# A one-core decode step (cached attention beside a gated MLP): z in 8 products per chunk, four wo chunks into the first accumulator, w_out dealt anew

## The chip, the cores and the metric

The kernel runs on 1 core of one Trainium2 chip. The metric is device time in microseconds (us) of one execution. Before the change it is 662.26 us (median of 3 runs, 662.09 to 662.38).

## The reference

For 4 batch rows of width 640, x is layer-normed to xn, and the result is x + attention(xn) + mixer(xn).

```python
q = (xn @ wq)                       # 640 -> 32 heads x 128, one query per row
p = softmax(q . k_cache / sqrt(128))  # k_cache: 4 x 32 x 4096 x 128, bf16
o = p . v_cache                     # v_cache: the same shape
A = o.reshape(4, 1, 4096) @ wo      # 4096 -> 640

z  = gelu_tanh(xn @ w_in)           # 640 -> 1728
z1, z2 = z[:, :864], layernorm(z[:, 864:])
B  = (z1 * (w_sp * z2 + b_sp)) @ w_out   # 864 -> 640; w_sp is 1 x 1, b_sp one number
out = x + A + B
```

The two caches are 134 MB each; wq, wo and the mixer's weights come to some 14 MB.

## The kernel before, in words

**Units.** The heads are taken in 4 groups of 8 (`NG`, `HG`), the batch rows one by one, so there are 16 units of K and 16 of V, 8.4 MB each: 128 partitions with 64 KB each. A tile `kv` of five slots of 32 KB per partition holds what is in flight; `place` (L159 to L166) says which two slots a unit takes. The sequence `seq` is K of units 0 to 3, then V and K in turn. `load_unit` (L179) issues a unit's load on SyncE's queue (SP), in one DMA or in the pieces of `cuts`. SP's queue is in order: a load waits for its slot to be free, and everything behind it waits too.

**K.** `emit_K` (L409) transposes an eighth of a unit on VectorE (L420, L429) into `kT_t`, a part of the tile `w_words`, and multiplies it on TensorE (L434) into the score tile S in PSUM. After the fourth K unit of a group, `softmax` makes p, and `z_fill` (L454) spreads it into `Zb`, also in `w_words`. `emit_V` (L497) multiplies V by it (L505).

**The prologue.** SP issues wq (slot 0 and 1) and w_in (slot 2), then pieces "a" and "b" of w_out (`load_piece`, L139), then K of unit 0. GpSimd's queue (POOL) issues a small load into the tile `walk` (L133) and the pieces "w", "s", "n", "m", "l" of w_out, each held behind the one before by `tc.issue_after`. w_out lies in `w_words` before K's transposes may write there: 95 partitions by `FC` = 26 columns of 640 numbers (a chunk of the contraction for each column). `PC` gives for each piece the partitions p0 to p1 with step st, the first chunk, the number of chunks n, and k and run, which say how the rows of w_out in DRAM are laid over partitions and chunks: `(r i c) n -> i r (c n)`, with i = k and c = run. Partitions that no piece covers stay zero from the memsets of L135 and L136.

**z.** For each of the 5 chunks of the contraction over 640, L343 multiplies xn by the columns of w_in in the order in which w_out's rows lie over partitions and chunks: 16 products per chunk (for pieces with `run == n`, one for each r), 80 in all, into two banks of PSUM (`zr_ps`), in six blocks of 32 partitions (`z_in`). The gelu (L351, ScalarE, 8 instructions) writes them into `z_f`, whose halves are z1 and z2. The layer norm's sums, the normalisation, the gate and the product run on VectorE and GpSimd (L363 to L381) over 32 * FC = 832 columns; L382 transposes the result in 32 x 32 blocks to `uT`. L395 multiplies it with w_out: 26 chunks by 2 halves of the output, 52 products into the accumulator `proj`, which already holds x (L288). K's first transpose may write `w_words` only after them.

**Slots.** w_in and z_f lie in slot 2. K of unit 2 goes to slots 2 and 3, so that its load waits for the product of L381 and for the transposes of K of unit 0 out of slot 3.

**The end.** Behind the last V, SP issues wo: groups 1, 2 whole and the last group (`NG - 1`) in pieces of chunks 0 to 4, 4 to 6, 6 to 7 and 7 to 8 (`load_wo`, L192). `emit_proj` (L551, its products at L548) adds groups 0 to 2 into `proj`, even chunks into rows 0 to 31 and odd ones into rows 32 to 63. The last accumulation into `proj` is that of group `NG - 2`, chunks 4 to 8. VectorE copies one half (`o_1`, L601) and adds the other (`o_q`, two instructions of L605). The last group's 8 chunks go by quarters of the output, 32 products, into an accumulator of their own, `last` (L608 to L613). L616 adds `last` and `o_q`, and two DMAs (L619) write the result.

**The walk.** Five loads of 4 bytes into `walk` (L569) stand on SP's queue between the loads of K of units 0 and 1, each waiting for an earlier DMA.

Of the kernel before, what the change touches and what calls it, by code (L numbers as in the profile page):

```python
# [8 lines left out]
ACT = mybir.ActivationFunctionType  # L9
# [3 lines left out]
BF16 = mybir.dt.bfloat16  # L13
# [3 lines left out]
def kernel(  # L17
# [19 lines left out]
    nc = tc.nc  # L37
# [5 lines left out]
    HG = 8  # L43
# [8 lines left out]
    NG = H // HG  # L52
# [1 line left out]
    G = HG * B  # L54
    F2 = B_w_in.shape[1]
    Fh = F2 // 2
    FC = 26

    PC = {"a": (32, 52, 2, 0, 18, 5, 18), "b": (0, 12, 1, 0, 14, 3, 14), "w": (16, 28, 2, 0, 19, 3, 19),
          "s": (60, 68, 1, 0, 23, 2, 23), "n": (68, 84, 2, 0, 17, 4, 17), "m": (84, 92, 2, 0, 1, 2, 1),
          "l": (92, 95, 1, 0, 26, 2, 13)}
    f_of, f_end = {}, 0
    for t, (p0, p1, st, _, n, _, _) in PC.items():
        f_of[t] = (f_end, f_end + len(range(p0, p1, st)) * n)
# [4 lines left out]
    NO2 = NOUT // NH  # L71
# [3 lines left out]
    const = ctx.enter_context(tc.tile_pool(name="const", bufs=1))  # L75
# [12 lines left out]
    def misc_ps(shape, dtype):  # L88
        misc_ctr[0] += 1
        return ps_m.tile(shape, dtype, tag="misc", name=f"misc{misc_ctr[0]}")  # L90
# [8 lines left out]
    n_w = (2 * NKT, (2 * TC + 1) * 16, NW * HG * 2, NW * HG * 2, NP // 2 + M)  # L99
    w_words = const.tile([P, max(sum(n_w), FC * NOUT // 2)], F32, name="w_words")  # L100
    w_part = [w_words[:, sum(n_w[:i]):sum(n_w[:i + 1])] for i in range(len(n_w))]
# [27 lines left out]
    w_in = at_slot(2, n_in).rearrange("p (c f) -> p c f", c=DC)  # L129
    nc.sync.dma_start(out=w_in, in_=B_w_in.rearrange("(p c) f -> p c f", c=DC))  # L130

    walk = const.tile([8, 138], BF16)
    sw = nc.gpsimd.dma_start(out=walk[:, 0:128], in_=B_w_out[0:8, 0:128].rearrange("(r i) n -> i r n", i=4))  # L133
    MS = 15 * NOUT // 2
    nc.vector.memset(w_words[:, 0:MS], 0.0)  # L135
    nc.gpsimd.memset(w_words[:, MS:FC * NOUT // 2], 0.0)  # L136
    w_out = w_words[:, 0:FC * NOUT // 2].bitcast(BF16).rearrange("p (c n) -> p c n", c=FC)

    def load_piece(eng, t):  # L139
        p0, p1, st, c0, n, k, run = PC[t]  # L140
        return eng.dma_start(out=w_out[p0:p1:st, c0:c0 + n].rearrange("p c n -> p (c n)"),
                             in_=B_w_out[f_of[t][0]:f_of[t][1], :].rearrange("(r i c) n -> i r (c n)", i=k, c=run))

    load_piece(nc.sync, "a")
    load_piece(nc.sync, "b")
    for t in ("w", "s", "n", "m", "l"):
        with tc.issue_after(sw.ins):
            sw = load_piece(nc.gpsimd, t)

    NB = 32 * FC  # L150
    z_at = n_in
# [117 lines left out]
    for q in range(4):  # L269
        nc.gpsimd.tensor_copy(out=SelE[32 * q:32 * q + 32, :, q % 2, :],  # L270
                              in_=b8[32 * q:32 * q + 32, 8:8 + HP, None].to_broadcast((32, HP, P // HG)))
# [10 lines left out]
                          in_=ident_f[:].rearrange("p (q x c) -> p q x c", q=2, c=C2))  # L282


    proj = ps_j.tile([64, 512], F32)
# [8 lines left out]
    for hf in range(2):  # L294
        for c in range(DC):
            for j in range(NG):
                n0 = j * HG * Dh + hf * 512
# [16 lines left out]
    w_z = w_in.rearrange("p c (a f) -> p c a f", a=2)  # L314
    zr_ps = [misc_ps([P, 2, 256], F32) for _ in range(2)]
# [2 lines left out]
    z_in = {(0, 0): ('b',), (0, 1): ('a',), (0, 2): ('n', 'm', 'l'), (1, 0): ('w',), (1, 1): ('s',), (1, 2): ('s',)}  # L318
    z_at_col, z_parts = {}, []
    for (bk, q), names in z_in.items():  # L320
        col, parts = 0, []
        for t in names:
            p0, p1, st, _, n, k, run = PC[t]
            x0, x1 = max(p0, 32 * q), min(p1, 32 * q + 32)
            m = len(range(x0, x1, st)) * n
            assert col + m <= 256
            src = w_z[:, :, :, f_of[t][0]:f_of[t][1]].rearrange("p d a (r i c) -> p d a r i c", i=k, c=run)
            dst = zr_ps[bk][32 * q:32 * q + 32, :, col:col + m]
            if x1 - x0 < p1 - p0:
                parts.append((dst, src[:, :, :, :, (x0 - p0) * k // (p1 - p0)]))  # L330
            elif run < n:
                d_i = dst.rearrange("p a (i f) -> p i a f", i=k)
                parts += [(d_i[:, i], src[:, :, :, :, i]) for i in range(k)]
            else:
                d_r = dst.rearrange("p a (i r c) -> p r a i c", i=k, c=n)
                parts += [(d_r[:, r], src[:, :, :, r]) for r in range(m // (k * n))]
            z_at_col[bk, q, t] = (col, m, n, PC[t][3], x0 - 32 * q, x1 - 32 * q, st)
            col += m
        z_parts.append(parts)
    for c in range(DC):  # L340
        for parts in z_parts:
# [4 lines left out]
    z_b = [ppool.tile([P, NB], BF16, tag="p", name=f"z_b{i}") for i in range(2)]  # L346
    zT = z_f[:, 0:2, :].rearrange("p a (i j) -> p a i j", j=32)
    nc.gpsimd.memset(z_f[:, 0:2, :], 0.0)
    for (bk, q, t), (col, m, n, c0, x0, x1, st) in z_at_col.items():
        rows = slice(32 * q, 32 * q + 32)  # L350
        nc.scalar.activation(out=zT[rows, :, c0:c0 + n, x0:x1:st],  # L351
                             in_=zr_ps[bk][rows, :, col:col + m].rearrange("p a (x c) -> p a c x", c=n),
                             func=ACT.Gelu_apprx_tanh)

    one_bf = const.tile([1, P], BF16)
    nc.vector.memset(one_bf[:], 1.0)
# [32 lines left out]

    for f0 in range(0, FC, 4):  # L390
        for hf in range(NH):
            for fc in range(f0, min(f0 + 4, FC)):
                nb = 32 if fc == 1 and hf == 0 else RW
# [139 lines left out]
    def emit_oT(g):  # L533
        om = state.pop(("om", g))
        oR = small.tile([P, B, HG], F32, tag="oR")
        nc.vector.tensor_reduce(out=oR[:], in_=om[:].rearrange("p b q c -> p b c q"), axis=AX.X, op=ALU.add)
        oT = small.tile([P, HG * RW + 2], BF16, tag="oT", bufs=3)
        nc.gpsimd.memset(oT[:], 0.0)  # L538
        nc.vector.tensor_tensor(out=oT[:, 1:1 + HG * RW].rearrange("p (c b h) -> p c b h", c=HG, h=NH)[:, :, :, 0],
                                in0=oR[:].rearrange("p b c -> p c b"),  # L540
                                in1=state.pop(("rinv", g))[:, None, :].to_broadcast((P, HG, B)), op=ALU.mult)
        state[("oT", g)] = oT

    def o_mul(dst, g, c, hf, n0, n1, start, stop):

        nb = 32 if start else RW
        c0 = RW * c + 1 - hf
        nc.tensor.matmul(dst[0:nb, 0:n1 - n0], lhsT=state[("oT", g)][:, c0:c0 + nb], rhs=wo_t[g][:, c, n0:n1],  # L548
                         start=start, stop=stop)

    def emit_proj(g, h2=range(2), stop=False):  # L551
        for h in h2:
            for hf in range(NH):
                for c in range(4 * h, 4 * h + 4):
                    o_mul(proj[32 * (c % 2):32 * (c % 2) + 32], g, c, hf, hf * NO2, (hf + 1) * NO2, False,
                          stop and hf == NH - 1 and c > HG - 3)
# [6 lines left out]
    for i, item in enumerate(seq):  # L563
# [13 lines left out]
        g, b = divmod(u, B)  # L577
# [17 lines left out]
    emit_sel(NG - 1)  # L595
    emit_proj(NG - 2, (0,))
    emit_oT(NG - 1)
    emit_proj(NG - 2, (1,), True)

    o_1 = ppool.tile([32, NO2], F32, tag="p", name="o_1")  # L600
    nc.vector.tensor_copy(out=o_1[:], in_=proj[0:32, 0:NO2])  # L601
    NQ = NO2 // 2
# [2 lines left out]
        nc.vector.tensor_tensor(out=o_q[32 * k:32 * k + 32, :], in0=proj[32:64, k * NQ:(k + 1) * NQ],  # L605
                                in1=o_1[:, k * NQ:(k + 1) * NQ], op=ALU.add)
    last = ps_l.tile([64, NQ], F32)
    for c in range(HG):  # L608
        for hf in range(NH):
            for k in range(2):  # L610
                n0 = hf * NO2 + k * NQ
                o_mul(last[32 * k:32 * k + 32], NG - 1, c, hf, n0, n0 + NQ, c == 0 and hf == 0,
                      c == HG - 1 and hf == NH - 1)  # L613

    o_bf = ppool.tile([64, NQ], BF16, tag="p", name="o_bf")
# [32 lines left out]
```

## Time and profile before

| | us |
|---|---|
| median of 3 runs (range) | 662.26 (662.09 to 662.38) |
| the profiled execution, its own time | 662.32 |
| its span, first to last instruction | 660.5 |
| TensorE / VectorE / ScalarE / GpSimd busy | 277.2 / 377.4 / 74.8 / 76.9 |
| bytes read from HBM | 282.25 MB, 427 GB/s over the span |
| granted TensorE clock, mean | 0.75 |

The profile shows one execution. Engines are PE (TensorE), PEld (its weight loads), DVE (VectorE), ACT (ScalarE), POOL (GpSimd) and SP (SyncE); a name with q is an engine's queue. The span is cut in 40 slices of 16.5 us; a digit of 9 is a busy share of 90% or more. The chain that ended last is followed back from the last instruction, each time to what released it. Times in the timeline are from the span's start; behind an instruction stands in brackets how long its engine was idle and what ended that. Beside the instructions the trace holds one record for each DMA packet (start, duration, bytes, queue) and one for each landing of a DMA on one of the 16 DMA engines; the numbers on single packets come from these.

### The profile page before, as it was taken

The page shows a single profiled execution, that of the slowest core. Times are in us where ns is not written, and L with a number is a line of the kernel's source. Part 1 is how long each engine was busy: PE and PEld are TensorE (multiplying, and loading weights), DVE is VectorE, ACT ScalarE, POOL GpSimd, SP SyncE. Part 2 cuts the span into 40 slices and gives each one's busy share as a digit, 9 for nine tenths or more (in the row PEclk, how much of TensorE's full clock was granted, in tenths as well). Part 3 has the DMA queues.
Part 4 walks back from the last instruction along what each step waited for, and adds up shares of the span by engine and source line. Part 5 has one row for each costly group of instructions (what it writes and reads, how often), then busy time and mean ns, then how long its engine had stood idle before and what let it go on. Part 6 is the DMA issues. An engine that isn't in the chain of part 4 may idle for free.

```text
span 660.5 us, 5606 instructions
## 1 busy us (share of the span) xinstructions
PE 277.2 (42%) x2329; PEld 106.6 (16%) x2329; DVE 377.4 (57%) x316; ACT 74.8 (11%) x144; POOL 76.9 (12%) x138
## 2 busy tenths in 40 slices
PE   0435566436052445334335062444507244244246
PEld 0222111112011121111112021111202112011012
DVE  4239999756191759718356192886619175485112
ACT  0310000431100000330200000033100000006200
POOL 7441000031100000130300000003110000003300
PEclk9759878668687697667859577776957779596769
DMA  9999999999999999999999999999999999999997
GB/s 369 444 446 442 407 430 439 441 438 437 426 425 442 429 420 443 438 426 437 434 429 441 442 417 434 433 433 438 438 429 433 418 437 442 433 442 433 400 433 309
DMA packets 6796, 282.60 MB, mean 428 GB/s; under 512 B 1080, under 2 KB 1344, under 8 KB 1602
## 3 DMA queue, kind: packets, MB, share of 16 engines
q1 hardware_dynamic: 6392, 281.58, 98.9%
q0 software_dynamic: 352, 0.66, 0.3%
q8 instruction: 18, 0.29, 0.2%
q14 instruction: 6, 0.05, 0.0%
q10 hardware_dynamic: 28, 0.01, 0.0%
HBM read 282.25 MB, written 0.01 MB: 427 GB/s over the span
## 4 chain that ended last, share of the span: by engine, by line
DMA 70%; DVE 12%; issue 12%; PE 3%; POOL 1%; ACT 1%; SPq 0%; DVEq 0%; POOLq 0%; ACTq 0%
DMA kv<-in_A_k_cache_dram 59%; DVE w_words L420 10%; DMA kv<-in_A_v_cache_dram 4%; DMA kv<-in_B_w_in_dram 4%; DMA kv<-in_A_wo_dram 4%; PE O L505 1%; PE proj L395 1%; DVE w_words L429 1%; POOL kv L379 0%; PE misc L343 0%; ACT kv L351 0%; DVE w_words L485 0%; POOL z_b L381 0%; SPq L194 0%; PE S L434 0%
## 5 line engine op out<-in xcount | busy, mean ns | idle before, releaser
L420 DVE STREAM_TRANSPOSE w_words<-kv 128x2048 f32<-128x2048 f32 x124 | 273.8, 2274 | 131.8 <-DMA kv<-in_A_k_cache_dram 128.7
L434 PE MATMUL S<-w_words,QZ 128*32 128x512 bf16 x1024 | 176.2, 473 | 269.0 <-DVE w_words L420 267.5
L434 PEld LDWEIGHTS <-QZ 128*32 128x32 bf16 x1024 | 57.3, 107 | 386.6 <-issue 324.5
L505 PE MATMUL O<-kv,w_words 128*32 128x512 bf16 x1024 | 72.0, 443 | 50.4 <-DMA kv<-in_A_v_cache_dram 40.6
L471 ACT ACTIVATE w_words<-w_words,MkE 32x128 bf16<-32x128 bf16 x120 | 60.9, 508 | 100.9 <-PE O L505 87.7
L514 DVE TENSOR_TENSOR om<-O,Mk 128x512 f32<-128x512 f32 x15 | 10.4, 692 | 83.8 <-PE O L505 83.8
L469 POOL TENSOR_SCALAR w_words<-w_words,MkE 32x128 bf16<-32x128 bf16 x60 | 43.1, 718 | 122.6 <-PE O L505 102.0
L479 ACT ACTIVATE w_words<-S,negmax 128x1024 bf16<-128x1024 f32 x4 | 4.5, 1114 | 413.1 <-DVE negmax L451 413.1
L505 PEld LDWEIGHTS <-w_words 128*32 128x32 bf16 x1024 | 32.8, 109 | 88.5 <-issue 59.0
L467 DVE TENSOR_SCALAR w_words<-w_words,MkE 32x128 bf16<-32x128 bf16 x76 | 24.9, 327 | 2.3
L403 POOL COPY QZ<-qT 32x32 bf16<-32x32 bf16 x16 | 5.0, 315 | 178.2 <-PE S L434 177.6
L515 DVE TENSOR_REDUCE R<-om 128x128 f32<-128x512 f32 x15 | 15.3, 1021 | 0.5
L490 POOL TENSOR_SCALAR rs<-MkB,rowsum 128x4 f32<-128x4 f32 x4 | 1.2, 296 | 120.8 <-ACT w_words L479 120.8
L485 DVE STREAM_TRANSPOSE w_words<-w_words 128x1024 bf16<-128x1024 bf16 (+1 forms) x8 | 9.6, 1240 | 5.6 <-ACT w_words L479 5.6
L538 POOL MEMSET oT<- 128x66 bf16 x4 | 0.5, 152 | 97.8 <-PE proj L548 97.8
L395 PE MATMUL proj<-w_words,z_b 128*8 128x320 bf16 (+1 forms) x52 | 6.5, 440 | 8.8 <-DVE z_b L382 8.8
L429 DVE STREAM_TRANSPOSE w_words<-kv 128x1024 f32<-128x1024 f32 x8 | 9.3, 1201 | 0.0
L517 DVE TENSOR_SCALAR R<-O,Mk 128x128 f32<-128x128 f32 x1 | 0.4, 351 | 12.7 <-PE O L505 12.7
L527 PE MATMUL misc<-R,SelX 128*128 128x512 f32 x8 | 4.5, 644 | 7.1 <-DVE R L515 5.5
L441 DVE TENSOR_REDUCE m<-S 128x1 f32<-128x1024 f32 x4 | 4.9, 1224 | 4.0 <-PE S L434 4.0
L298 PE MATMUL q<-kv,xnT 128*32 128x512 bf16 x40 | 4.5, 630 | 6.2 <-DMA walk<-in_B_w_out_dram 6.2
L492 PE MATMUL misc<-rs,SelE 128*128 128x4 f32 x8 | 2.3, 364 | 10.4 <-POOL rs L490 10.4
(102 smaller groups left out, 97.6 us busy)
## 6 DMA issues: line engine op xcount, KB each, us to landing
kv<-in_A_k_cache_dram SPq DMA_DIRECT2D x4, 4096.0 KB
kv<-in_A_v_cache_dram SPq DMA_DIRECT2D x1, 6144.0 KB
kv<-in_A_wq_dram SPq DMA_DIRECT2D x1, 5120.0 KB
kv<-in_A_wo_dram SPq DMA_DIRECT2D x3, 1280.0 KB
kv<-in_B_w_in_dram SPq DMA_DIRECT2D x1, 2160.0 KB
kv<-in_A_v_cache_dram SPq DMA_DIRECT2D x1, 2048.0 KB
kv<-in_A_wo_dram SPq DMA_DIRECT2D x1, 640.0 KB
kv<-in_A_wo_dram SPq DMA_DIRECT2D x1, 320.0 KB
```

The source lines that it names most:

```text
L395: nc.tensor.matmul(proj[r0:r0 + nb, 0:NO2], lhsT=uT[:, u0:u0 + nb], rhs=w_out[:, fc, hf * NO2:(hf + 1) * NO2], start=(fc == 1 and hf == 0) ...
L403: nc.gpsimd.tensor_copy(out=QZ[r0:r0 + 32, :, :, :, 8 + 8 * hp], in_=qT[32 * g:32 * g + 32, NE * hp:NE * hp + NE].rearrange("p e a b -> p ...
L420: nc.vector.transpose(kT.rearrange("p (t r) -> p t r", r=32), kw)
L429: nc.vector.transpose(kT_v[:, x], kw[:, TC * x:TC * x + TC])
L434: nc.tensor.matmul(S_ps[32 * q:32 * q + 32, i], lhsT=QZ[:, b, 2 * kh + w, e, w0:w0 + 32], rhs=kb[:, i, :, e, :, w], start=(b == 0 and k < ...
L467: nc.vector.tensor_scalar(out=dst, in0=src, scalar1=mk, scalar2=None, op0=ALU.mult)
L469: nc.gpsimd.tensor_scalar(out=dst, in0=src, scalar1=mk, scalar2=None, op0=ALU.mult)
L471: nc.scalar.activation(out=dst, in_=src, func=ACT.Copy, scale=mk)
L485: nc.vector.transpose(pT_t[:, j0:j1, :], blocks)
L505: nc.tensor.matmul(O_ps[32 * q:32 * q + 32, :, :], lhsT=Zb[b % 2][:, w].rearrange("p h c -> p (h c)"), rhs=vv[:, w * 4 * Dh:(w + 1) * 4 * ...
L514: nc.vector.tensor_tensor(out=om4[:], in0=O_ps[:], in1=Mk4[:, :, None].to_broadcast((P, 4, Dh)), op=ALU.mult)
L515: nc.vector.tensor_reduce(out=R, in_=om4[:].rearrange("p c d -> p d c"), axis=AX.X, op=ALU.add)
```

## The change

Three things, and what follows from them.

1. *w_out is dealt anew.* `FC` goes from 26 to 24. Piece b takes 13 chunks in place of 14, w 18 in place of 19, s 24 in place of 23, l 24 in place of 26; a and n stay. m was 4 partitions by 1 chunk (4 rows of w_out) and becomes 1 partition by 20 chunks (20 rows). Ahead of m a load of 256 bytes into `walk` is put on POOL's queue. All of the mixer's instructions over 32 * FC columns go from 832 to 768, and L395 from 52 to 48 products.
2. *z in 8 products per chunk.* For pieces with `run == n` the products no longer follow the order of the chunks; neighbouring pieces of one block are multiplied in one product, in the order of w_in's columns. The gelu reads the PSUM in permuted order; where the permutation has too many dimensions for one instruction it is two, one for each half of z: 12 gelus in place of 8 (b, a, n and w have two each).
3. *The end.* The chunks 0 to 4 of the last wo group go into `proj`, in 8 products of 320 columns; `o_1` and `o_q` follow behind these. `last` takes chunks 4 to 8, 16 products in place of 32.

```diff
--- before.py
+++ after.py
@@ -54,13 +54,13 @@
     G = HG * B
     F2 = B_w_in.shape[1]
     Fh = F2 // 2
-    FC = 26
-
-
-
-    PC = {"a": (32, 52, 2, 0, 18, 5, 18), "b": (0, 12, 1, 0, 14, 3, 14), "w": (16, 28, 2, 0, 19, 3, 19),
-          "s": (60, 68, 1, 0, 23, 2, 23), "n": (68, 84, 2, 0, 17, 4, 17), "m": (84, 92, 2, 0, 1, 2, 1),
-          "l": (92, 95, 1, 0, 26, 2, 13)}
+    FC = 24
+
+
+
+    PC = {"a": (32, 52, 2, 0, 18, 5, 18), "b": (0, 12, 1, 0, 13, 3, 13), "w": (16, 28, 2, 0, 18, 3, 18),
+          "s": (60, 68, 1, 0, 24, 2, 24), "n": (68, 84, 2, 0, 17, 4, 17), "m": (88, 89, 1, 0, 20, 1, 20),
+          "l": (92, 95, 1, 0, 24, 2, 12)}
     f_of, f_end = {}, 0
     for t, (p0, p1, st, _, n, _, _) in PC.items():
         f_of[t] = (f_end, f_end + len(range(p0, p1, st)) * n)
@@ -129,7 +129,7 @@
     w_in = at_slot(2, n_in).rearrange("p (c f) -> p c f", c=DC)
     nc.sync.dma_start(out=w_in, in_=B_w_in.rearrange("(p c) f -> p c f", c=DC))
 
-    walk = const.tile([8, 138], BF16)
+    walk = const.tile([8, 266], BF16)
     sw = nc.gpsimd.dma_start(out=walk[:, 0:128], in_=B_w_out[0:8, 0:128].rearrange("(r i) n -> i r n", i=4))
     MS = 15 * NOUT // 2
     nc.vector.memset(w_words[:, 0:MS], 0.0)
@@ -143,9 +143,12 @@
 
     load_piece(nc.sync, "a")
     load_piece(nc.sync, "b")
-    for t in ("w", "s", "n", "m", "l"):
+    for t in ("w", "s", "n", "-", "m", "l"):
         with tc.issue_after(sw.ins):
-            sw = load_piece(nc.gpsimd, t)
+            if t == "-":
+                sw = nc.gpsimd.dma_start(out=walk[0:1, 138:266], in_=B_w_out[0:1, 128:256])
+            else:
+                sw = load_piece(nc.gpsimd, t)
 
     NB = 32 * FC
     z_at = n_in
@@ -318,24 +321,32 @@
     z_in = {(0, 0): ('b',), (0, 1): ('a',), (0, 2): ('n', 'm', 'l'), (1, 0): ('w',), (1, 1): ('s',), (1, 2): ('s',)}
     z_at_col, z_parts = {}, []
     for (bk, q), names in z_in.items():
-        col, parts = 0, []
+        col, parts, plain = 0, [], []
         for t in names:
             p0, p1, st, _, n, k, run = PC[t]
             x0, x1 = max(p0, 32 * q), min(p1, 32 * q + 32)
-            m = len(range(x0, x1, st)) * n
+            xs = len(range(x0, x1, st))
+            m = xs * n
             assert col + m <= 256
-            src = w_z[:, :, :, f_of[t][0]:f_of[t][1]].rearrange("p d a (r i c) -> p d a r i c", i=k, c=run)
+            f0, f1 = f_of[t]
+            src = w_z[:, :, :, f0:f1].rearrange("p d a (r i c) -> p d a r i c", i=k, c=run)
             dst = zr_ps[bk][32 * q:32 * q + 32, :, col:col + m]
             if x1 - x0 < p1 - p0:
                 parts.append((dst, src[:, :, :, :, (x0 - p0) * k // (p1 - p0)]))
+                form = "x c"
             elif run < n:
                 d_i = dst.rearrange("p a (i f) -> p i a f", i=k)
                 parts += [(d_i[:, i], src[:, :, :, :, i]) for i in range(k)]
+                form = "x c"
             else:
-                d_r = dst.rearrange("p a (i r c) -> p r a i c", i=k, c=n)
-                parts += [(d_r[:, r], src[:, :, :, r]) for r in range(m // (k * n))]
-            z_at_col[bk, q, t] = (col, m, n, PC[t][3], x0 - 32 * q, x1 - 32 * q, st)
+                assert not plain or plain[-1][1:] == (col, f0)
+                plain.append((plain[0][0] if plain else (col, f0), col + m, f1))
+                form = "x c" if run == n and xs == k else "r i c"
+            z_at_col[bk, q, t] = (col, m, n, PC[t][3], x0 - 32 * q, x1 - 32 * q, st, form)
             col += m
+        if plain:
+            (col0, f0), col1, f1 = plain[-1]
+            parts.append((zr_ps[bk][32 * q:32 * q + 32, :, col0:col1], w_z[:, :, :, f0:f1]))
         z_parts.append(parts)
     for c in range(DC):
         for parts in z_parts:
@@ -346,11 +357,18 @@
     z_b = [ppool.tile([P, NB], BF16, tag="p", name=f"z_b{i}") for i in range(2)]
     zT = z_f[:, 0:2, :].rearrange("p a (i j) -> p a i j", j=32)
     nc.gpsimd.memset(z_f[:, 0:2, :], 0.0)
-    for (bk, q, t), (col, m, n, c0, x0, x1, st) in z_at_col.items():
+    for (bk, q, t), (col, m, n, c0, x0, x1, st, form) in z_at_col.items():
         rows = slice(32 * q, 32 * q + 32)
-        nc.scalar.activation(out=zT[rows, :, c0:c0 + n, x0:x1:st],
-                             in_=zr_ps[bk][rows, :, col:col + m].rearrange("p a (x c) -> p a c x", c=n),
-                             func=ACT.Gelu_apprx_tanh)
+        src = zr_ps[bk][rows, :, col:col + m]
+        dst = zT[rows, :, c0:c0 + n, x0:x1:st]
+        if form == "x c":
+            pairs = [(dst, src.rearrange("p a (x c) -> p a c x", c=n))]
+        else:
+            k = PC[t][5]
+            pairs = [(dst[:, a].rearrange("p c (i r) -> p c i r", i=k),
+                      src[:, a].rearrange("p (r i c) -> p c i r", i=k, c=n)) for a in range(2)]
+        for z_out, z_src in pairs:
+            nc.scalar.activation(out=z_out, in_=z_src, func=ACT.Gelu_apprx_tanh)
 
     one_bf = const.tile([1, P], BF16)
     nc.vector.memset(one_bf[:], 1.0)
@@ -595,7 +613,10 @@
     emit_sel(NG - 1)
     emit_proj(NG - 2, (0,))
     emit_oT(NG - 1)
-    emit_proj(NG - 2, (1,), True)
+    emit_proj(NG - 2, (1,))
+    for c, hf in ((0, 0), (1, 0), (0, 1), (1, 1), (2, 0), (3, 0), (2, 1), (3, 1)):
+        p = c % 2
+        o_mul(proj[32 * p:32 * p + 32], NG - 1, c, hf, hf * NO2, (hf + 1) * NO2, False, c > 1 and hf == 1)
 
     o_1 = ppool.tile([32, NO2], F32, tag="p", name="o_1")
     nc.vector.tensor_copy(out=o_1[:], in_=proj[0:32, 0:NO2])
@@ -605,11 +626,11 @@
         nc.vector.tensor_tensor(out=o_q[32 * k:32 * k + 32, :], in0=proj[32:64, k * NQ:(k + 1) * NQ],
                                 in1=o_1[:, k * NQ:(k + 1) * NQ], op=ALU.add)
     last = ps_l.tile([64, NQ], F32)
-    for c in range(HG):
+    for c in range(4, HG):
         for hf in range(NH):
             for k in range(2):
                 n0 = hf * NO2 + k * NQ
-                o_mul(last[32 * k:32 * k + 32], NG - 1, c, hf, n0, n0 + NQ, c == 0 and hf == 0,
+                o_mul(last[32 * k:32 * k + 32], NG - 1, c, hf, n0, n0 + NQ, c == 4 and hf == 0,
                       c == HG - 1 and hf == NH - 1)
 
     o_bf = ppool.tile([64, NQ], BF16, tag="p", name="o_bf")
```

## The prediction

> **What bounds the kernel now.** I read the page's slices and queues first, then the chain that ended last, then the timeline of the tail, and last the packet records.
>
> ```profile
> span 660.5 us, 5606 instructions
> DMA  9999999999999999999999999999999999999997
> q1 hardware_dynamic: 6392, 281.58, 98.9%
> q0 software_dynamic: 352, 0.66, 0.3%
> q8 instruction: 18, 0.29, 0.2%
> DMA 70%; DVE 12%; issue 12%; PE 3%; POOL 1%; ACT 1%; SPq 0%; DVEq 0%; POOLq 0%; ACTq 0%
> ```
>
> The DMA row is 9 in 39 of 40 slices. The records say it sharper. Within an engine one packet follows another after some 3 ns, so the records fall into 16 chains, one for each DMA engine (where two end within a few ns they can be swapped). From 4 to 656 us all 16 are busy, in every stretch that I summed; a packet of 64 KB takes 2.42 us. The chains' last packets end between 655.99 and 656.94 us, 656.57 in the mean, and the last landing is at 657.40. So the time is the load of the last DMA engine, plus some 2 us before it, plus the tail. The busiest compute engine, DVE, has 57%.
>
> ```profile
> 43.85 0.04 issue
> 43.90 6.50 PE proj L395 x52
> 50.40 0.95 PE S L434 x8
> ...
> 53.61 2.28 DVE w_words L420
> 55.90 0.02 SPq L186
> 55.92 0.04 issue
> 55.96 0.03 SPq L186
> 55.99 0.04 issue
> 56.03 27.31 DMA kv<-in_A_k_cache_dram
> ```
>
> In the chain, z's path ends in the load of K of unit 2 being issued at 56.03. The 27.31 us behind it are not all its own: the records show the first engine done with K of unit 1 only at 58.7, the last at 63.5, and all 16 go on at once. wq's load was issued at 0.72 and moved its first packet at 1.74, 1.0 us later; so the issue is some 1.7 us earlier than needed.
>
> ```profile
> 654.23 1.26 PE L548 MATMUL proj<-kv,oT 128*8 128x320 bf16 x16 [1.22 <-DMA kv<-in_A_wo_dram]
> 655.53 0.48 DVE L601 COPY o<-proj 32x320 f32<-32x320 f32 x1 [1.62 <-PE proj L548]
> 655.81 1.94 PE L548 MATMUL last<-kv,oT 128*32 128x160 bf16 x32 [0.32 <-DMA kv<-in_A_wo_dram]
> 656.04 0.65 DVE L605 TENSOR_TENSOR o_q<-proj,o 32x160 f32<-32x160 f32 x2
> 657.79 0.32 DVE L616 TENSOR_TENSOR o_bf<-last,o_q 64x160 bf16<-64x160 f32 x1 [1.10 <-PE last L548]
> ```
>
> In the tail DVE waits 1.10 us for `last`: the pieces of wo end last, not the products.
>
> **z's path.** *Products:* 80 become 40 with the same columns, in 2.58 us of the chain (25.12 to 27.70). Bounds: nothing (columns decide) and half, -1.3 us (each product's own cost decides); I take -1.0, as the 10 products of 4 columns had nearly nothing but their own cost. *Gelu:* its line runs from 151 ns (8 columns) to 474 ns (360), so some 145 ns each beside the columns; 4 more are +0.6. *Elementwise:* 832 to 768 columns is -7.7% of L364, L365, L379, L380, L381 and L382 (1.58 + 1.03 + 3.16 + 1.03 + 1.94 + 1.06 = 9.8 us): -0.75. *L395:* 4 of 52 products in 6.50 us: -0.5. Sum -1.65 us, bounds -0.65 and -1.95 with the products' bounds: K of unit 2 is issued at 54.1 to 55.4. *On the path that sets the end: nothing*, as all 16 engines have K of unit 1 to move until 58.7 at least. The cover would be gone at an issue after 57.7.
>
> [...]
>
> **Issue.** SP's queue carries as many DMAs as before, in the same order. POOL's gets one more, the 256 bytes ahead of m: an issue took 0.6 us (five pieces in 2.88), so m and l leave 0.6 later, and POOL's own work behind them too, into a gap of 3.59 us that POOL has before L216. l's landing, the last of w_out, was complete at 41.93 and becomes some 42.5; L395 is ready for it at 43.90 - 1.2 = 42.7 (without its own 0.5). If l is late, L395 waits for it, and the 1.7 us above cover that. POOL's memset L136 goes from 3.05 to 2.5 us; SP's wait (4.3 us at L141) is for DVE's L135, which stays.
>
> **The DMA engines' loads.** This is where a time can change. The bytes are the same; their place is not. Durations of packets: 23040 bytes 855 ns, 24320 902, 29440 1091, 17920 667, 16640 620, 21760 808. The records show a on 5 engines (2 packets each), b on 3 (4 each, two of these seen to hold 2 of a), w on 3 (2 each), s on 2 (4 each), n on 4 (2 each), m on 2 (one of 102 ns each), l on one (all 6). In us:
>
> - engines with a and b: 1.71 + 2.67 = 4.38; b's 16640 bytes make it 4.19 (-0.19)
> - with s: 4.36; 30720 bytes, between the rows of 29440 and 32768 (1213), are 1138 ns: 4.55 (+0.19)
> - with l: 3.72; 15360 bytes, 573 ns by the slope of those rows: 3.44 (-0.28)
> - with w: 1.80 to 1.71 (-0.09); a alone and n: unchanged
> - m: 0.10 on two engines; one keeps nothing (-0.10), the other has 25600 bytes, 0.95 (+0.85)
>
> The second load is instruction fetches: 18 records of 16 KB (queue 8), some 256 PE instructions apart. One holds an engine 1.55 us: that of 99.03 took 1.03, and the packet behind it 2.96 in place of 2.42. They go to the lightly loaded engines, as far as the chains can be told apart, both engines of m among them; those with s, b and l get none. The change takes 104 PE instructions away: a product and a weight load each for 40 of z, 4 of L395 and 8 of L548. The last fetch, at 648.89, came with 4565 of 4701 recorded PE instructions started; with 4597 in all it falls into the last 16 products or out of the program. That is -1.55 us on one engine, the one that was earliest then by 0.7 us.
>
> What this makes of the last engine: perfect balance would end at the mean, 656.57, less 1.55 / 16, so -0.47 us at best. At worst m's new engine was among the last: +0.85. Followed to the end, the latest chain carries a and b (it gets -0.19); others that end within 0.1 to 0.2 us of it carry n or w (0 to -0.09), and those with s were some 0.3 before it (+0.19). So the next engine ends some 0.1 us earlier: I take -0.1. Both of m's engines ended some 0.2 us before the last: the one with the fetch of 648.9 can take m (0.85 - 1.55), the other would be last by 0.65. The rows do not tell which it will be; the engine freed of a fetch is as likely as the other, and the rest of the working does not hang on it but through this rival.
>
> **Tail.** The piece of chunks 0 to 4 lands at 655.77. The 8 products into `proj` are 8 x 79 ns (16 in 1.26) = 0.63, to 656.44; `o_1` 0.48 and `o_q` 0.65, with gaps of 0.04, to 657.65. L616 starts at 657.79 on `last`, whose chunks 4 to 6 land at 656.62, behind the 8 products. So 0.14 us of cover is left of 1.10: 0 us, bounds 0 and +0.3 (a product at its own 299 ns rather than pipelined would add more, but 16 in a row were not). The last 4 products (0.32) and the out DMA stay.
>
> **Sum.** 662.32 (span 660.5 and 1.8 around it) + 0 - 0.1 + 0 = 662.2. The profiled execution is 0.06 over the median.
>
> **Rivals.**
>
> *m's engine becomes the last* (26%): +0.65 from the balance above, up to +0.85: 663.0 to 663.2. For it: both of m's engines ended close to the last. Against: one fetch less on one of them.
>
> *The dealing does not come out as meant* (7%), the slower side. On POOL's queue the walk and the five pieces lie on 4, 3, 2, 4, 2 and 1 engines, 16 in sum and, as far as the chains tell, all different: they seem to take their engines in turn, so that every execution starts alike. It decides at the new 256 bytes: if they take any number of engines but one, l moves on to other engines from one execution to the next, and where it meets a and b, that engine has 4.19 + 3.44 = 7.6 in place of 4.4 us: +3.2, 665.4. Against: the loads of 4 bytes at L569 each take one engine. [...]
>
> *z's path was on the critical path after all* (4%): -1.65 us, 660.6. For it: the chain runs through it. Against: no gap in any engine's packets at 58 to 64 us.
>
> *The tail loses its cover* (5%): `o_q` late by up to 0.3: 662.5.
>
> **How the numbers follow.** The likeliest case, balance within the ends -0.47 to +0.4, has 58%: 661.8 to 662.7 around 662.2. The range takes in the tail and m's engine and leaves out the two cases of 7 and 4%: 661.7 to 663.2. 0.2% of this time is 1.3 us, about what a measurement can tell from no change. Faster by more: 4%, z's path alone. Slower by more: 7% from the dealing and 1% for m's engine meeting a late fetch as well. Within: 88%.
>
> **What would show it.** In the profile after: DMA still 9 in all slices but the last; K of unit 2 issued at 54 to 55.4 with no gap behind; 40 products at L343 in 1.3 to 2.6 us; 12 gelus; 17 fetches on queue 8, or an 18th after 655; `o_q` ending by 657.7 and L616 released by PE; the last landing at 657.0 to 657.5. A last landing near 658.1 with m's engine last would be the first rival, ends of engines spread over 3 us the second.

## The result: 6.0 us slower, because one DMA engine ends last by itself

The changed kernel takes 668.26 us (median of 5 runs, 668.11 to 668.33), the kernel before 662.26. The ratio is 1.009, with a 95% interval from 1.0079 to 1.0102. The forecast was 662.2 with a range from 661.7 to 663.2, so it was wrong, and not only in size: it saw no change, and the kernel is slower.

The page after, the same lines as were shown of before (span, DMA row, POOL's queue q0, instruction fetches q8):

```profile
span 666.2 us, 5510 instructions
DMA  9999999999999999999999999999999999999995
q0 software_dynamic: 384, 0.68, 0.3%
q8 instruction: 18, 0.29, 0.2%
```

The DMA row is full until the last slice, which falls from 7 to 5: some engines have nothing left to do while another still works. The landings say how much. Those of the last piece of wo lay within 0.91 us before (656.49 to 657.40). After they lie within 5.38 us (657.68 to 663.07), and 15 of the 16 are in by 659.4; one engine is 3.65 us later than all others. The last landing is 5.67 us later than before, and the span 5.73 us longer: all but 0.06 us of the longer span lies in front of that landing. (The other 0.2 us of the profiled executions' difference lie outside the span.)

POOL's queue has 32 packets more. The DMA issues of the kernel after show the two loads that were meant for one engine each, and l (columns: queue, count, size, us from issue to landing), and below them l in the kernel before:

```profile
w_words<-in_B_w_out_dram POOLq DMA_DIRECT2D x1, 90.0 KB, 37.1
...
w_words<-in_B_w_out_dram POOLq DMA_DIRECT2D x1, 25.0 KB, 21.5
...
walk<-in_B_w_out_dram POOLq DMA_DIRECT2D x1, 0.2 KB, 17.2
```

```profile
w_words<-in_B_w_out_dram POOLq DMA_DIRECT2D x1, 97.5 KB, 33.5
```

In the packet records the 256 bytes are 16 packets of 16 bytes and m is 16 packets of 1600 bytes (67 ns each), as many as there are engines (that each engine took one is a reading; no record names the engine). l is smaller than before (90 KB for 97.5), but takes 37.1 us in place of 33.5. Its six packets of 15360 bytes should take 573 ns each by the forecast; the first did, the others took 713 to 739. Beside them two of the 16 engines show 64 KB packets of K at 2.7 to 3.0 us in place of 2.42, from 25 to 43 us, as long as l runs.

The chain of the kernel after, in its prologue (start, duration, what):

```profile
8.82 37.12 DMA w_words<-in_B_w_out_dram
45.95 0.35 issue
46.30 5.99 PE proj L413 x48
...
57.92 28.29 DMA kv<-in_A_k_cache_dram
```

l's landing now holds the product with w_out (L413, L395 before) until 46.30, and K of unit 2 is issued at 57.92. In the timeline of the tail, the add (L637, L616 before) now follows `o_q` with no idle time before it:

```profile
661.49 0.71 PE L566 MATMUL proj<-kv,oT 128*8 128x320 bf16 x8 [0.30 <-DMA kv<-in_A_wo_dram]
662.24 0.48 DVE L622 COPY o<-proj 32x320 f32<-32x320 f32 x1 [2.58 <-PE proj L566]
662.29 1.13 PE L566 MATMUL last<-kv,oT 128*32 128x160 bf16 x16
662.75 0.65 DVE L626 TENSOR_TENSOR o_q<-proj,o 32x160 f32<-32x160 f32 x2
663.50 0.32 DVE L637 TENSOR_TENSOR o_bf<-last,o_q 64x160 bf16<-64x160 f32 x1
```

### The profile page after: what moved, and what is told of

Same layout as the page of the kernel before. It is cut to its first block, busy times and chain, and to the rows that moved or that the text cites. A ratio compares the mean times of both kernels' runs of the same rounds, so it can differ in the third digit from the quotient of the medians.

```text
span 666.2 us, 5510 instructions
## 1 busy us (share of the span) xinstructions
PE 280.0 (42%) x2277; PEld 107.1 (16%) x2277; DVE 377.3 (57%) x316; ACT 74.9 (11%) x148; POOL 76.2 (11%) x139
## 4 chain that ended last, share of the span: by engine, by line
DMA 72%; DVE 13%; issue 12%; PE 3%; POOL 0%; ACT 0%; SPq 0%; DVEq 0%; ACTq 0%
DMA kv<-in_A_k_cache_dram 59%; DVE w_words L438 10%; DMA w_words<-in_B_w_out_dram 6%; DMA kv<-in_A_v_cache_dram 4%; DMA kv<-in_A_wo_dram 4%; PE O L523 1%; PE proj L413 1%; DVE w_words L447 1%; DVE w_words L135 1%; DVE w_words L503 0%; POOL w_words L141 0%; PE S L452 0%; DVE w_words L485 0%; DVE m L459 0%; ACT w_words L497 0%
## 5 line engine op out<-in xcount | busy, mean ns | idle before, releaser
L452 PE MATMUL S<-w_words,QZ 128*32 128x512 bf16 x1024 | 178.8, 478 | 268.0 <-DVE w_words L438 266.1
L523 PE MATMUL O<-kv,w_words 128*32 128x512 bf16 x1024 | 73.8, 451 | 51.6 <-DMA kv<-in_A_v_cache_dram 34.3
L523 PEld LDWEIGHTS <-w_words 128*32 128x32 bf16 x1024 | 33.5, 111 | 91.1 <-issue 62.6
L413 PE MATMUL proj<-w_words,z_b 128*8 128x320 bf16 (+1 forms) x48 | 6.0, 438 | 10.9 <-DMA w_words<-in_B_w_out_dram 10.9
```

The lines of the kernel that those rows point to most:

```text
L413: nc.tensor.matmul(proj[r0:r0 + nb, 0:NO2], lhsT=uT[:, u0:u0 + nb], rhs=w_out[:, fc, hf * NO2:(hf + 1) * NO2], start=(fc == 1 and hf == 0) ...
L452: nc.tensor.matmul(S_ps[32 * q:32 * q + 32, i], lhsT=QZ[:, b, 2 * kh + w, e, w0:w0 + 32], rhs=kb[:, i, :, e, :, w], start=(b == 0 and k < ...
L523: nc.tensor.matmul(O_ps[32 * q:32 * q + 32, :, :], lhsT=Zb[b % 2][:, w].rearrange("p h c -> p (h c)"), rhs=vv[:, w * 4 * Dh:(w + 1) * 4 * ...
```

## The experiments

The theory: POOL's pieces take their engines in turn, as the prediction supposed from the chains of packets, and the 256 bytes and m, in 16 packets each, do not move the place in the turn where the next piece begins. l then falls two engines earlier than before, on the first of the two that used to carry m. That engine takes an instruction fetch of 16 KB three times in a run (the 1st, the 9th and the 17th; its lag shows them, see below). A second part, theory B below, is for the slow packets of l (713 to 739 ns) and of K beside it (2.7 to 3.0 us): it looks for their cause in the partitions that l is written to. No record shows which engine writes to which partitions, so this part is a supposition. The rivals: the tail, z's path, the new sizes of the pieces. All comparisons are with runs of the kernel before on the same chip.

**The dealing repaired.** Everything of the change stays, but m's 20 rows lie on 4 partitions by 5 chunks and the 256 bytes are gone.

```diff
-"m": (88, 89, 1, 0, 20, 1, 20)
+"m": (84, 92, 2, 0, 5, 2, 5)
-    for t in ("w", "s", "n", "-", "m", "l"):
+    for t in ("w", "s", "n", "m", "l"):
...
```

> The change with m's 20 rows on 4 partitions by 5 chunks (two shares) and without the 256 bytes, so that l falls on its engine of before; everything else of the change stays. Theory (the 6 us are l on another engine): 661.8 to 662.5 us, the 15360-byte packets all at 573 ns, the landing of w_out before 43 us. Rival (the late o_1 and o_q, or z's path and the gelus, cost the time): it stays at 667 to 668.5.

Measured: 662.57 us against 662.30 (ratio 1.0003, 0.9994 to 1.0013). All six packets of l take 573 ns, and the last landing is at 657.59. The 6 us are gone with z's products, the gelus, 24 chunks and the new tail all still in place, so those rivals fall. Two points of the expectation missed: the time is 0.07 us above its range, and w_out was complete at 44.26, not before 43. The chain of the repaired kernel shows the second, and that K of unit 2 is issued at 55.74, in time all the same:

```profile
8.39 35.87 DMA w_words<-in_B_w_out_dram
44.61 2.07 PE proj L410 x14
55.74 27.45 DMA kv<-in_A_k_cache_dram
```

**The kernel before with m as one run.** The opposite test: nothing of the change but one contiguous run of m, with m's four rows.

```diff
-"m": (84, 92, 2, 0, 1, 2, 1)
+"m": (88, 89, 1, 0, 4, 1, 4)
```

> The kernel before with m's 4 rows on one partition (one contiguous run of 2560 numbers) and nothing else changed. Theory: m is split over 16 engines and l moves to another engine; 666.5 to 669 us, with l's packets slowed. Rival (the new sizes of b, s, l, the gelus or the tail matter): 662.1 to 662.5 as before.

Measured: 668.60 us against 662.30 (1.0095, 1.008 to 1.011). m is 16 packets of 320 bytes; l's packets, 620 ns before, take 636 and then 815 to 835, one 1274. The whole slowdown comes back with four rows of w_out and without any other part of the change. The profile shows the same signs, here l's landing and the product that waits for it:

```profile
w_words<-in_B_w_out_dram POOLq DMA_DIRECT2D x1, 97.5 KB, 37.4
...
46.05 6.55 PE L395 MATMUL proj<-w_words,z_b 128*8 128x320 bf16 x52 [10.79 <-DMA w_words<-in_B_w_out_dram]
```

**l on other partitions.** The changed kernel, with l moved from partitions 92 to 94 to 84 to 86. The order of POOL's loads and l's bytes stay. That l should run undisturbed on just these partitions is an assumption of theory B; no run before this one shows it.

```diff
-"l": (92, 95, 1, 0, 24, 2, 12)
+"l": (84, 87, 1, 0, 24, 2, 12)
```

> [...] Theory A (l's bytes and the instruction fetches on one engine are all): unchanged, 668.0 to 668.5. Theory B (besides, two engines that write to the same partitions slow each other): l's packets back at 573 ns, no 64 KB packet of the prologue slowed to 2.7 to 3.0 us, and 665.0 to 665.9 us (the engine of before ended 0.2 us before the last one and gets 3.4).

Measured: 665.60 us against 662.30 (1.005, 1.0035 to 1.0065). All of l's packets are back at 573 ns, and the long rows of slowed K packets are gone; five single ones over 2.5 us are left before 58 us (19 in the changed kernel). One engine is still last alone: the last landings run from 656.44 to 657.62 for 15 of them and 660.55 for the 16th. The forecast of theory B came true. Moving l took away 2.66 us of the loss (668.26 to 665.60), with the slow packets; 3.03 are left over the repaired kernel (662.57), put down to the load.

**The same slowing without the load.** The repaired kernel, with l on its engine of before but on partitions 84 to 86, and m on 88 to 94. That l should be slowed there is the same assumption.

```diff
-"m": (84, 92, 2, 0, 5, 2, 5)       "l": (92, 95, 1, 0, 24, 2, 12)
+"m": (88, 96, 2, 0, 5, 2, 5)       "l": (84, 87, 1, 0, 24, 2, 12)
```

> [...] Loads of all engines as in the repaired version. Theory A: 661.8 to 662.5. Theory B: l's packets at some 720 ns and the K packets of two engines slowed while l runs; each loses some 2 to 3.5 us and the time is 663.5 to 666.

Measured: 666.02 us against 662.30 (1.0055, 1.0038 to 1.0072), which is 3.45 over the repaired version. l's packets take 644 to 736 ns, and 64 KB packets of 2.7 to 3.0 us stand beside them until 41.5 us, when l ends. The time is at the upper end of theory B's range, 0.02 us over it. Bytes, order and shapes of the loads are those of the repaired kernel; only the partitions that l is written to differ (and m's). What moving m's 25.6 KB does was not measured apart.

**256 bytes alone.** The kernel before with that load ahead of m.

> The kernel before with the load of 256 bytes put ahead of m and nothing else. If a load that is split over all 16 engines does not move the engines of those behind it: 662.2 to 662.5, l's packets at 620 ns. If it does move them: l on another engine, l's packets slowed and 664 to 669 us.

Measured: 662.55 us against 662.26 (1.0006, 0.9997 to 1.0015), 0.05 us above the expected range, with l's packets at 620 ns as before. POOL's queue has 384 packets for 352, and nothing shows that l changed its place. In the change, then, the load does nothing for the dealing; it is m's one run, which alone takes 668.60 us, that takes away the two places that m used to fill.

**The parts of the change alone.** Three runs: the repaired kernel with the old tail; the kernel before with the new tail alone; and with z's 8 products and permuted gelus alone. The tail's edit, in the form undone:

```diff
-    emit_proj(NG - 2, (1,))
-    for c, hf in ((0, 0), (1, 0), (0, 1), (1, 1), (2, 0), (3, 0), (2, 1), (3, 1)):
...
+    emit_proj(NG - 2, (1,), True)
```

> The repaired dealing (m on two engines, no 256 bytes) and z in 8 products, with the end of the kernel before (all eight chunks of the last wo group into their own accumulator). If the late o_1 and o_q cost what the repaired profile shows (L616's successor starts at 658.05 where the last landing of 657.59 would allow some 657.98): 0.05 to 0.1 us less than the repaired version's 662.57, so 662.4 to 662.6. If the tail is the whole of the remaining 0.3 us: 662.2 to 662.3.

> The kernel before with the four chunks into the first accumulator alone. Cover 0.14 us by the forecast: 662.2 to 662.4, L616 released by PE. If the cover is gone: 662.4 to 662.6, L616 released by DVE.

> z in 8 products and the permuted gelus alone, with the old dealing of w_out (26 chunks) and the old end. If z's path is hidden by the DMA: 662.1 to 662.4. If it counted after all: 660.5 to 661.5 faster, or over 662.8 if the products and gelus make it longer and K of unit 2 late.

Measured, against 662.26: repaired with the old tail 662.47 (1.0004, 0.9995 to 1.0013), tail alone 662.32 (1.0002, 0.9993 to 1.001), z alone 662.59 (1.0005, 0.9996 to 1.0013). None can be told from the kernel before. z alone lies 0.19 us above its expected range and below the 662.8 of the other case; the interval does not tell it from either side. The old tail came out 0.1 us below the repaired version, as expected, but on another chip and with intervals of some 0.6 us to either side, so that gain is not shown. Two signs in the profiles are sharper than the times. With the tail alone the chain's end is DVE's, as expected for a cover that is gone, though the time is that of a cover that holds; the last landing is at 657.44, and the add starts 0.44 us behind it, where it was 0.39 (657.40 to 657.79):

```profile
656.62 0.49 DVE o L604
657.11 0.02 issue
657.13 0.32 DVE o_q L608
657.45 0.01 issue
657.46 0.33 DVE o_q L608
...
657.88 0.32 DVE o_bf L619
```

With z alone the chain's end is the last piece of wo again:

```profile
633.78 23.67 DMA kv<-in_A_wo_dram
657.45 0.04 issue
657.49 0.32 PE last L563 x4
657.81 0.02 issue
657.84 0.32 DVE o_bf L631
```

No version beat the kernel before, and its profile leaves little to win by balance: by its landings, perfectly even engines would end some 0.4 us earlier (an estimate, 0.06%).

## Why the prediction was wrong, point by point

- *What bounds the kernel* was right. All that mattered was the load of the last DMA engine, and the time moved by about what its last landing moved (+6.0 and +5.7 us).
- *The step that failed* is "the other has 25600 bytes, 0.95 (+0.85)" in the engines' loads, and with it the 256 bytes as one load of one engine. Neither was one load of one engine: both were 16 packets. m's own were 67 ns each; the harm, by the runs, was that l lost its place. The sum had no term for that: it left l's engine as it was. With m as one run the kernel before takes 668.60 us, and with m on two engines the changed kernel takes 662.57.
- *The rival that came true* was the dealing not coming out as meant, at 7%. Its condition was half right: the 256 bytes were 16 packets, but alone they move nothing (662.55 us). m's run does (668.60), and the rival asked only about the 256 bytes: m, a longer run of the same kind, was put on one engine without a question. The row I set against it, the loads of 4 bytes on one engine, was a bad witness: a run of two numbers stayed whole, one of 128 did not, and no row of before showed a long run on one partition. The record of an issuing instruction holds the shape of its destination: it is 16 elements of 16 bytes for the 256 bytes, 16 of 1600 for m's run of 12800 numbers and 16 of 320 for one of 2560, but one element for a load of 4 bytes. So the runs were already split when the loads were issued, and each became 16 packets.
- *Its price* was +3.2 us and it cost 6.0. It was worked out for l meeting a and b. In fact l met the fetches: in the changed kernel the last engine falls further behind the others at three of them, those of 50.3 us (its lag behind the first from 5.37 to 6.77 us), 328.5 (4.55 to 6.09) and 637.9 (4.07 to 5.55). An engine with l's 3.44 us besides these makes the kernel 3.03 us slower than the repaired one. The sum fits if that is the engine that ends last in the repaired kernel too, which also steps back at the 17th fetch: it gives up m's two packets of 244 ns and gets l's 3.44 us and 0.07 of the spread m, +3.02. And it had no term for the partitions that l is written to: 2.66 us (668.26 to 665.60).
- *"Other engines from one execution to the next"* was wrong. In the changed kernel the walk, w, s, n and l fill 14 places of the supposed turn in place of 16 (4, 3, 2, 4 and 1), and still five runs agree within 0.22 us. So if POOL's loads take their engines in turn, the turn seems to begin anew with each execution.
- *z's path.* The products took 2.74 us (25.29 to 28.03), not less than the 2.58 of before, but these two are not alike: the granted clock fell from 1.0 to 0.5 at 24.23 us in the changed kernel and at 25.74 before. With z alone, where it fell at 25.79, the 40 products took 2.23 us; and where it was 0.5 from their start nearly to their end, 80 took 2.92 (256 bytes alone) and 40 took 2.74. So the form saved some 0.2 to 0.35 us: the -1.0 was too large, and the bound by columns is the nearer one. The gelus took 2.82 us for 12, against 2.62 for 8: +0.2 in place of +0.6. The elementwise work fell by 0.65 us, near the 0.75 worked out, and L395 by 0.5, as worked out. Of the sum of -1.65, -1.15 lie before L395; by the transpose's end (43.84 to 43.75) it was -0.1, with the products begun 0.17 later. All of it was hidden, as said; z alone is no faster.
- *Cover of K of unit 2.* I had l complete at 42.5 and the load issued by 55.4, with 57.7 as the limit. It was 57.92, past the limit. The records show it as a gap of some 0.6 us, from 60.7 to 61.3, on one engine that was ahead; the last engine has none there. In the repaired kernel it is 55.74.
- *Tail.* The 8 products took 0.71 us, not 0.63, and from `o_q`'s end to the add there is 0.1 us more (663.40 to 663.50), which I had put at nothing. Together they use up the 0.14 us of cover: L616 was released by DVE in every version with the new tail. It costs some 0.05 us by the profiles, inside the bounds of 0 and 0.3.
- *Fetches.* 18, the last at 661.08, so after 655 as foreseen, though with 51 PE instructions still to start and not 32. The last engine shows no further lag from it.
- *Balance.* The repaired version gives what the sum was for: forecast 662.2, measured 662.57. The time is 0.4 above the forecast, inside the range. Its last landing is 0.19 us later than before. m's two engines had ended some 0.2 us before the last and get 0.37 each (6400 bytes twice in place of 2560 once), which fits, though the engine was not traced to the end.

## What to carry to other kernels

Where all DMA engines are busy all the time, as here from 4 to 656 us, ask not only how many bytes a piece has but which engine carries them: the changed kernel and its repaired version load the same w_out and take 668.26 and 662.57 us. Here the packets followed from the shape: m's four rows of w_out were 2 packets of 2560 bytes on four partitions, and 16 packets of 320 bytes as one contiguous run on one partition (662.30 and 668.60 us). So before a piece's shape is changed, count how many engines it takes and which ones the pieces behind it then get. A look at the packet sizes on a queue, one line per size, shows it at once.

## What the runs showed of the hardware

Whether l ran undisturbed hung on two things together, its place behind the other pieces and the partitions that it was written to. On partitions 92 to 94 its packets of 15360 bytes took 573 ns where m had two shares (repaired kernel), and five of the six took 713 to 739 ns where m was 16 packets (changed kernel), with 64 KB packets of K at 2.7 to 3.0 us beside them in place of 2.42. On 84 to 86 it was the other way round: 644 to 736 ns where m had two shares, 573 ns where m was 16 packets. Moving l to other partitions removed the slowing in one kernel (668.26 to 665.60 us, -2.66) and brought it about in another, in which m was moved too (662.57 to 666.02, +3.45). That two engines which write to the same partitions slow each other is the author's explanation and is not shown; no record says which engine writes to which partitions.

The load of 256 bytes, in 16 packets, left l's packets at 620 ns and the time at 662.55 us (662.26 without). By the dealing's theory it does not change where the loads behind it go; the runs cannot tell whether it takes no place in the turn or a full turn of 16.
